# The beginning of a chunked linear-attention kernel: step 0's r and k in two transfers, and four r products behind the masks

## The chip, the core and the metric

The kernel runs on one core of a Trainium2 chip. The core has a matrix engine (TensorE, PE in the rows), two elementwise engines (VectorE, DVE; GpSimd, POOL), an activation engine (ScalarE, ACT) and a sync engine that issues transfers (SyncE, SP). Each engine runs its own instructions strictly in the order in which they were written and waits on semaphores for the others. Sixteen DMA engines move data between HBM and on-chip memory; SP and ACT both issue such transfers here, each on a queue of its own. The metric is the device time of one execution in microseconds (us).

## What is computed

A linear attention with decay over 768 tokens, for 4 batches and 8 heads of 48 dimensions, and then a mixture of experts over its output:

```python
for t in range(S):                        # S = 768
    cur = einsum('bhd,bhe->bhde', u * k[t], v[t])
    y[t] = einsum('bhd,bhde->bhe', r[t], state + cur)
    state = w[:, :, None] * state + einsum('bhd,bhe->bhde', k[t], v[t])
x = y as (3072 tokens, 384)
# tokens with x @ w_skip > 0 go to the expert argmax(x @ w_gate):
out = x + gate * (relu(x @ w1[e]) @ w2[e])
```

## The kernel before, in words

The attention is cut into chunks of 64 tokens. A step handles one chunk of two batches and all heads; there are 24 steps (NT), 12 for each pair of batches. The experts follow, about the second half of the time; the splitting of their weights and the routing run beside the steps.

A step n needs r and k from one transfer `dm{n}` (448 KB, both halves in one tile; three such buffers) and v from two transfers (`load_v`). Then:

- `prep_r(n)` (line 446, VectorE): `rd = r * table`, the table `w_d` of powers of the decay being built by VectorE at the start (lines 371 to 393) from the small input `wd`, loaded to `w_in`. `grow(1..3)` (line 362) make its three other quarters, which steps 1 to 3 need first. Four `rd` buffers.
- `bonus(n)`: `rd * u`, two heads at a time: two short activations on ScalarE (line 464), and one instruction on GpSimd (line 456) for the other half; in step 0 VectorE takes that half.
- `prep_k(n)` (line 469): `kd = k / table`, on GpSimd, for steps 0 and 1 on VectorE. Its end frees the buffer of `dm{n}` for `dm{n+3}`.
- `scores(n)` (line 496, TensorE): 16 small products into the one bank pair `ps_p`; `mask_scores(n)` (lines 508, 509, VectorE): two copies out of it, which have to be done before `scores(n+1)` writes it again.
- `within(n)` (line 550), `turn_x(n-1)` (line 619, transposes of the output of the step before), `turn_k` (482), `state` (520), `across(n)` (566): all on TensorE, in this order. ScalarE copies the result of `turn_x(n-1)` out of PSUM (line 623, "the x copy"). The first product of `across(n)` waits for that copy by a dependency written out by hand: `behind(mm, turned_x[n - 1])`. In every fourth step `gate_four` (636), which reads the copied x, stands between `state` and `across`.

The order in the loop over n decides what stands where on each engine. Before the change, iteration n is: `scores(n+1)`; `prep_r`, `bonus`, `prep_k` of step n+3; `within(n)`; `mask_scores(n+1)`; `turn_x(n-1)`, `turn_k(n+1)`, `state(n)`; `across(n)`. Iteration 0 prepares step 3 at its end. `warm` (line 271) fills TensorE with products of ones, at the very start and in a few gaps. `blank` (294) clears halves of the v buffers ahead of their first load.

Of the kernel before, what the change touches and what calls it, by code (L numbers as in the profile page):

```python
# [9 lines left out]
F32 = mybir.dt.float32  # L10
# [29 lines left out]
ADV = NB * NHP  # L40
BIG = 4 * N
NVK = 6
NWARM = 15
EARLY = 16
HURRY = 20
TURN = 9
# [14 lines left out]
def tile_wkv_moe(  # L61
# [199 lines left out]
    with ExitStack() as actx:  # L261
# [7 lines left out]
        def warm(k, to=ps_l):  # L269
            for _ in range(k):  # L270
                nc.tensor.matmul(to, ones[:, :P], ones, start=True, stop=True)
# [4 lines left out]
        NPW = 9  # L276
        pw = tab.tile([DR, NPW, 4 * NHP], F32, name="pw")
        w_in = tab.tile([DR, 4 * NHP], F32, name="w_in")
        nc.sync.dma_start(out=w_in, in_=wd)
        ub_sb = tab.tile([DR, NHP], F32, name="ub_sb")  # L280
        nc.scalar.dma_start(out=ub_sb, in_=ub)

# [9 lines left out]
        def blank(n, eng):  # L292
            for g in range(2):
                eng.memset(v_of(n)[g * C : (g + 1) * C, 1 - g], 0.0)

        def load_rk(n):
            d = ld.tile([DR, 2, NB * NHP * C], F32, tag="dm", name=f"dm{n}", bufs=3)
            nc.sync.dma_start(out=d.rearrange("p s (q c) -> p s q c", c=C), in_=dm[n // NSTEP, n % NSTEP])
            loaded[n] = (d, v_of(n))

        def load_v(n, k=2):
# [22 lines left out]
        nc.gpsimd.memset(am[0], 0.0)  # L324
        nc.gpsimd.memset(am[1], 0.0)
        nc.vector.memset(ps_s, 0.0)
        blank(0, nc.vector)

        def lower(name, op):
            t = tab.tile([P, C], I8, name=name)  # L330
# [12 lines left out]

        below = lower("below", ALU.is_gt)
        eye = lower("eye", ALU.is_equal)
        for j in range(1, 4):
            blank(j, nc.gpsimd)

        def behind(ins, name, reason="other rows of the array write the same quadrants"):
# [9 lines left out]
        def grow(sub, eng, after=None):  # L359
            if sub:  # L360
                src, j = (0, 6) if sub == 1 else (sub - 2, 7)
                ins = eng.tensor_tensor(
                    w_d[:, sub].rearrange("p s h c -> p (s h) c"),
                    w_d[:, src].rearrange("p s h c -> p (s h) c"),
                    pw[:, j, : 2 * NHP].unsqueeze(2).to_broadcast([DR, 2 * NHP, C]),
                    ALU.mult,
                )
                if after is not None:
                    behind(ins, after.ins.name, "r and k go first where both engines wait")
# [73 lines left out]
        def prep_r(n):  # L443
            d = loaded[n][0][:, 0].rearrange("p (b h c) -> p b h c", b=NB, h=NHP)
            rd = wk.tile([DR, NB, NHP, 2, C], F32, tag="rd", name=f"rd{n}", bufs=4)
            ins = nc.vector.tensor_tensor(  # L446
                rd[:, :, :, 0], d, w_d[:, n % NSUB, 0][:, None].to_broadcast([DR, NB, NHP, C]), ALU.mult
            )
            rds[n] = rd
            return ins  # L450

        def bonus(n, hps, eng=None):
            rd = rds[n]
            if eng is not None:
                h = slice(hps[0], hps[-1] + 1)
                eng.tensor_tensor(  # L456
                    rd[:, :, h, 1],
                    rd[:, :, h, 0],
                    uw[:, h][:, None, :, None].to_broadcast([DR, NB, len(hps), C]),
                    ALU.mult,  # L460
                )
                return
            for hp in hps:
                nc.scalar.activation(rd[:, :, hp, 1], rd[:, :, hp, 0], AF.Copy, scale=uw[:, hp : hp + 1])  # L464

        def prep_k(n, eng=None, after=None):
            d = loaded[n][0][:, 1].rearrange("p (b q) -> p b q", b=NB)
            kds[n] = wk.tile([DR, NB, NHP, C], F32, tag="kd", name=f"kd{n}", bufs=3)
            ins = (eng or nc.gpsimd).tensor_tensor(  # L469
                kds[n].rearrange("p b h c -> p b (h c)"),  # L470
                d,
                w_d[:, n % NSUB, 1].rearrange("p h c -> p (h c)")[:, None, :].to_broadcast([DR, NB, NHP * C]),
                ALU.mult,
            )
            if after is not None:
                behind(ins, after.ins.name, "r goes first where both engines wait")
            return ins
# [11 lines left out]
        def scores(n):  # L489
            kd, rd = kds[n], rds[n]  # L490
            for j in range(4):
                b, jj = divmod(j, 2)
                for a, g in FOUR:
                    h = slice(a * C, a * C + D)
                    hp = 2 * jj + g
                    mm = nc.tensor.matmul(  # L496
                        ps_p[g * C : (g + 1) * C, a, j * P : (j + 1) * P],
                        kd[h, b, hp, :],
                        rd[h, b, hp].rearrange("p s c -> p (s c)"),
                        start=True,  # L500
                        stop=True,
                    )
            return mm
# [414 lines left out]
        setup = setup_routes()  # L918
        prep_r(0)
        bonus(0, (0, 1))  # L920
        bonus(0, (2, 3), nc.vector)
        prep_k(0, nc.vector)
        scores(0)
        grow(1, nc.vector)
        square(7, nc.gpsimd)
        square(8, nc.gpsimd)
        prep_r(1)
        bonus(1, (0, 1))
        turn_k(0)
        bonus(1, (2, 3))  # L930
        k1 = prep_k(1, nc.vector)
        mask_scores(0)
        warm(4)
        state(0)
        grow(2, nc.gpsimd, k1)
        prep_k(2, after=prep_r(2))
        bonus(2, (0, 1, 2, 3))
        grow(3, nc.gpsimd)
        for n in range(NT):
            four = n % 4 == 0 and n > 0  # L940
            if 0 < n < NT - 4 and n % 2 == 0:
                load_v(n + 4)
            if n + 1 < NT:
                scores(n + 1)
            if 0 < n < NT - 3:
                prep_r(n + 3)
                bonus(n + 3, (0, 1))
                bonus(n + 3, (2, 3), nc.gpsimd)
                prep_k(n + 3)
            if n - 1 in WSPLIT:  # L950
                split_lo(0, WSPLIT.index(n - 1), nc.gpsimd)
            if 0 < n and n + 6 < NT:
                load_rk(n + 6)
            if n == NT - 2:
                step_route(4)
            else:
                tick()
            within(n)
            if n == NT - 1:
                vctx.close()  # L960
                scr.append(lctx.enter_context(tc.tile_pool(name="scr", bufs=4, side="right", reuse_waits="tile")))
                first = begin(0, "vkv", xhl0)
            if n + 1 < NT:
                mask_scores(n + 1)
                tick()
            if n > 0:
                turn_x(n - 1)
                if (n + 1) % NSTEP < NSTEP - 1 and n + 1 < NT:
                    turn_k(n + 1)
                state(n)  # L970
            if four:
                gate_four(n // 4 - 1)
            warm(FILL.get(n, 0))
            tick(0 if n < HURRY else 6)
            if n == NT - 1:
                next(first)
            if n == NT - 1:
                gate_four(n // 4)
            across(n)
            if n == 0:  # L980
                turn_k(1)
                prep_r(3)
                bonus(3, (0, 1))
                bonus(3, (2, 3), nc.gpsimd)
                prep_k(3)
                load_rk(6)
            if n == NT - 1:
                gate_back(n // 4)
            if n % NSUB == NSUB - 1 and n % NSTEP < NSTEP - 1:
                keep_state(n)  # L990
            if n == NT - 2:
                turn(ps_l[:, :DM].rearrange("p (c q) -> p c q", q=P), 0, xhl0[:, 0], xhl0[:, 1])
            if n != NSTEP:
                step_route(2)
            if n == NSTEP + 1:
                gate_back(n // 4 - 1)
            if four and n != NSTEP:
                gate_back(n // 4 - 1)
            if n < NT - 3 or n == NT - 1:
                step_route(4)  # L1000
            if n == NT - 1:
                step_route(4)
                tick(6)
                next(first)
                turn_x(n)
            step_route(1)
            tick(1 if n + 1 < NT else 6)
            if n in ends:
                routes.append([route(ends[n], n), 0, n])
            if 1 <= n < 5:  # L1010
                next(setup, None)
            if n in (1, 2):
                blank(n + 3, nc.gpsimd)
            if n in RAW0:
                load_expert(0, RAW0.index(n), 12)
            for j in RAW1.get(n, ()):
                load_expert(1, j, 6)
            for j in RAW2.get(n, ()):
                load_expert(2, j, 6)
            if n in WSPLIT:  # L1020
                split_hi(0, wpool, WSPLIT.index(n))
# [356 lines left out]
```

## Time and profile before

| | us |
|---|---|
| three timed runs, median (lowest to highest) | 271.28 (269.43 to 272.1) |
| the profiled execution, own time | 266.43 |
| its span, first to last instruction | 264.6 |
| TensorE busy, of that span | 251.7 (95%) |
| VectorE, ScalarE, GpSimd busy | 170.6, 139.4, 110.8 |
| granted TensorE clock, mean | 0.994 |

The page of the profile gives for each engine the busy time, then the span in 40 slices, then the chain of work that ended last, followed back from the end, and the costliest groups of instructions. For this change the first 35 us matter, and there the timelines of the single engines. A timeline row is: start, duration, engine, line, operation, tile written and tile read, number of instructions, and in brackets the idle time ahead of it with what ended it. A chain row is: start, duration on the chain, what. An operand is given as partitions x elements.

### The profile page before, as it was taken

What the parts mean: (1) busy time and instruction counts of PE and PEld (TensorE: products, weight loads), DVE (VectorE), ACT (ScalarE), POOL (GpSimd) and SP (SyncE); (2) the same over time, 40 slices, a digit from 0 to 9 for tenths busy, and PEclk for the clock granted to TensorE, in tenths of its full rate; (3) what the DMA queues carried; (4) which work ended last, traced back from release to release, by engine and by line L of the source; (5) the groups of instructions that cost most, each with busy time, mean ns of one, the idle gap of its engine ahead of it and who ended that gap; (6) DMA issues with size and microseconds to landing.
All of it is one profiled execution on the core that took longest, in us unless ns stands there. A gap on an engine that the chain in (4) does not pass through costs nothing.

```text
span 264.6 us, 8597 instructions
## 1 busy us (share of the span) xinstructions
PE 251.7 (95%) x3579; PEld 225.5 (85%) x3581; DVE 170.6 (64%) x382; ACT 139.4 (53%) x315; POOL 110.8 (42%) x128
## 2 busy tenths in 40 slices
PE   7799998989999999999999999999999999999990
PEld 2578887778888888877789999999999999999990
DVE  7768555568664877737865967948659477494300
ACT  2566565656766756444773916637258174491200
POOL 8579554474765655501778151220310403105011
PEclk9999999999999999999999999999999999999997
DMA  6998699988997888496399979185291670101000
GB/s 159 245 254 257 196 257 245 274 216 242 254 265 215 246 250 266 103 345 203 108 305 285 330 215 386 54 296 231 57 398 60 223 301 18 30 0 35 11 32 24
DMA packets 20864, 52.21 MB, mean 197 GB/s; under 512 B 3556, under 2 KB 10224, under 8 KB 20816
## 3 DMA queue, kind: packets, MB, share of 16 engines
q1 hardware_dynamic: 18240, 46.42, 58.2%
q0 software_dynamic: 2048, 5.14, 6.2%
q8 instruction: 30, 0.49, 0.8%
q14 instruction: 18, 0.15, 0.2%
q10 hardware_dynamic: 528, 0.02, 0.1%
HBM read 43.77 MB, written 8.36 MB: 197 GB/s over the span
## 4 chain that ended last, share of the span: by engine, by line
PE 85%; DMA 7%; DVE 2%; issue 1%; ACT 1%; SPq 1%; POOL 0%; POOLq 0%; DVEq 0%
PE ps_p L178 11%; PE ps_y L178 11%; PE ps_l L168 11%; PE ps_p L496 8%; PE ps_y L550 7%; PE ps_s L520 6%; PE ps_p L168 5%; PE ps_x L168 5%; PE ps_y L566 5%; DMA dm<-in_dm_dram 4%; PE ps_t L619 4%; PE ps_l L482 3%; DMA raw<-in_w_dram 2%; PE ps_t L636 2%; PE ps_y L233 2%
## 5 line engine op out<-in xcount | busy, mean ns | idle before, releaser
L187 POOL DMA_INDIRECT out_dram<-xg,sid x16 | 23.7, 1478 | 89.8 <-DVE xg L183 79.8
L129 DVE TENSOR_TENSOR wlo<-raw,whi 128x512 fp32r<-128x512 f32 x84 | 54.0, 685 | 2.1 <-ACT whi L124 2.0
L124 ACT CAST whi<-raw 128x512 fp32r<-128x512 f32 x96 | 54.7, 626 | 0.0
L446 DVE TENSOR_TENSOR rd<-dm,w_d 112x512 f32<-112x512 f32 x24 | 17.7, 740 | 17.9 <-PE ps_y L566 15.6
L168 PE MATMUL ps_l<-x,whi 128*128 128x232 f32 x168 | 28.9, 274 | 0.0
L469 POOL TENSOR_TENSOR kd<-dm,w_d 112x512 f32<-112x512 f32 x22 | 28.1, 1278 | 1.0 <-DVE rd L446 1.0
L496 PE MATMUL ps_p<-rd,kd 48*64 48x128 f32 x768 | 26.4, 273 | 1.5 <-issue 0.8
L138 POOL DMA_INDIRECT xg<-out_dram,gid x16 | 19.3, 1204 | 19.7 <-DMA raw<-in_w_dram 13.4
L456 POOL TENSOR_TENSOR rd<-rd,uw 112x256 f32<-112x256 f32 x21 | 12.9, 615 | 33.1 <-DVE rd L446 23.3
L168 PEld LDWEIGHTS ps_l<-x,whi 128*128 128x128 f32 x168 | 25.5, 192 | 0.0
L464 ACT ACTIVATE rd<-rd,uw 112x128 f32<-112x128 f32 x52 | 18.0, 396 | 11.2 <-DVE rd L446 10.8
L496 PEld LDWEIGHTS ps_p<-rd,kd 48*64 48x64 f32 x768 | 20.9, 133 | 3.3 <-issue 1.4
L168 PE MATMUL ps_l<-x,wlo 128*128 128x232 f32 x84 | 23.2, 276 | 0.0
L172 ACT ACTIVATE hh<-ps_p 128x464 fp32r<-128x464 f32 x7 | 3.9, 559 | 33.1 <-PE ps_p L168 33.1
L550 PE MATMUL ps_y<-vkv,am 128*64 128x96 f32 x384 | 21.1, 252 | 0.1
L508 DVE COPY_PREDICATED am<-below,ps_p 128x512 f32<-128x512 int8 x24 | 17.7, 736 | 4.7 <-PE ps_p L496 4.3
L550 PEld LDWEIGHTS ps_y<-vkv,am 128*64 128x64 f32 x384 | 16.6, 136 | 4.2 <-issue 2.9
L520 PE MATMUL ps_s<-vkv,kt 128*48 128x96 f32 x352 | 19.4, 251 | 0.8 <-issue 0.8
L623 ACT COPY x<-ps_t 128x384 f32<-128x384 f32 x23 | 11.0, 478 | 16.0 <-PE ps_t L619 15.9
L178 PE MATMUL ps_p<-whi,hh 128*128 128x384 f32 x56 | 19.4, 347 | 0.0
L178 PE MATMUL ps_y<-whi,hh 128*104 128x384 f32 x56 | 18.9, 338 | 0.0
L178 PE MATMUL ps_p<-whi,hl 128*128 128x384 f32 x56 | 18.9, 337 | 0.0
(239 smaller groups left out, 591.2 us busy)
## 6 DMA issues: line engine op xcount, KB each, us to landing
raw<-in_w_dram SPq DMA_DIRECT2D x16, 768.0 KB, 7.9
dm<-in_dm_dram SPq DMA_DIRECT2D x24, 448.0 KB, 5.3
raw<-in_w_dram SPq DMA_DIRECT2D x24, 256.0 KB, 5.5
raw<-in_w_dram SPq DMA_DIRECT2D x12, 512.0 KB, 5.5
out_dram<-xt SPq DMA_DIRECT2D x26, 192.0 KB, 4.3
vkv<-in_tok_dram SPq DMA_DIRECT2D x22, 192.0 KB, 4.5
vkv<-in_tok_dram SPq DMA_DIRECT2D x4, 96.0 KB, 6.5
out_dram<-xt SPq DMA_DIRECT2D x4, 96.0 KB, 4.3
```

Source lines behind the costliest of these rows:

```text
L124: nc.scalar.copy(wsp[e][0][:, s], raw[e][:, s])
L129: eng.tensor_tensor(lo[:, s], raw[e][:, s], hi[:, s].bitcast(F32), ALU.subtract)
L138: ins = nc.gpsimd.indirect_dma_start(out=xg[:m], out_offset=None, in_=out[:rows], in_offset=bass.IndirectOffsetOnAxis(ap=gid[:m, q : q + 1 ...
L168: nc.tensor.matmul(ph, w1[a][:, c, fs], x[:, c, b, :], start=(k == 0), stop=(k == 3 * NCC - 1))
L178: nc.tensor.matmul(py, a, b[:, f, :], start=(k == 0), stop=(k == 3 * NFC - 1))
L187: ins = nc.gpsimd.indirect_dma_start(out=out, out_offset=bass.IndirectOffsetOnAxis(ap=sid[:m, q : q + 1], axis=0), in_=xs.pop(q)[:m], in_o ...
L446: ins = nc.vector.tensor_tensor(rd[:, :, :, 0], d, w_d[:, n % NSUB, 0][:, None].to_broadcast([DR, NB, NHP, C]), ALU.mult)
L464: nc.scalar.activation(rd[:, :, hp, 1], rd[:, :, hp, 0], AF.Copy, scale=uw[:, hp : hp + 1])
L469: ins = (eng or nc.gpsimd).tensor_tensor(kds[n].rearrange("p b h c -> p b (h c)"), d, w_d[:, n % NSUB, 1].rearrange("p h c -> p (h c)")[:, ...
L496: mm = nc.tensor.matmul(ps_p[g * C : (g + 1) * C, a, j * P : (j + 1) * P], kd[h, b, hp, :], rd[h, b, hp].rearrange("p s c -> p (s c)"), st ...
L520: nc.tensor.matmul(s[a * C : a * C + D, j * 2 * D : (j + 1) * 2 * D], kt[:, j, a, :], v[:, j, a], start=i == 0 and j == 0, stop=True, skip ...
L550: nc.tensor.matmul(ps_y[b * C : (b + 1) * C, a, jj * 2 * D : (jj + 1) * 2 * D], am[n % 2][:, a, j * C : (j + 1) * C], v[:, j, a], start=jj ...
```

## The change

- `w_in` is loaded on ScalarE's queue, ahead of `ub_sb`, no longer on SP's; SP begins with r of step 0, then k of step 0, as two transfers of 224 KB where there was one of 448 KB.
- `prep_k(0)` is made in two halves (one per batch), with VectorE's half of step 0's bonus between them. `blank(0)` goes from VectorE to GpSimd, and `blank(2)` and `blank(3)` go behind `prep_k(1)`.
- `prep_k(1)` goes from VectorE to GpSimd, so `mask_scores(0)` directly follows `prep_r(1)` on VectorE; `grow(2)` goes from GpSimd to VectorE, behind that mask. All four bonuses of step 1 are together on ScalarE.
- `warm`: 13 products at the start where there were 15; 3 and 2 around `state(0)` where there were 4.
- In iterations 1 to 4 (`LEAD = 5`) the preparation of step n+3, steps 4 to 7, stands behind `mask_scores(n+1)`; before it stood ahead of it. It still stands ahead of `turn_x(n-1)`.

```diff
-NWARM = 15
+LEAD = 5
+NWARM = 13
...
-        nc.sync.dma_start(out=w_in, in_=wd)
+        nc.scalar.dma_start(out=w_in, in_=wd)
...
-            nc.sync.dma_start(out=d.rearrange("p s (q c) -> p s q c", c=C), in_=dm[n // NSTEP, n % NSTEP])
+            for s in (slice(0, 1), slice(1, 2)) if n == 0 else (slice(0, 2),):
+                nc.sync.dma_start(
+                    out=d[:, s].rearrange("p s (q c) -> p s q c", c=C), in_=dm[n // NSTEP, n % NSTEP, :, s]
+                )
...
-        blank(0, nc.vector)
...
-        for j in range(1, 4):
+        for j in range(2):
             blank(j, nc.gpsimd)
...
         prep_r(0)
         bonus(0, (0, 1))
+        prep_k(0, nc.vector, part=slice(0, 1))
         bonus(0, (2, 3), nc.vector)
-        prep_k(0, nc.vector)
+        prep_k(0, nc.vector, part=slice(1, 2))
         scores(0)
+        turn_k(0)
         grow(1, nc.vector)
         square(7, nc.gpsimd)
         square(8, nc.gpsimd)
-        prep_r(1)
-        bonus(1, (0, 1))
-        turn_k(0)
-        bonus(1, (2, 3))
-        k1 = prep_k(1, nc.vector)
+        k1 = prep_k(1, after=prep_r(1))
+        for j in range(2, 4):
+            blank(j, nc.gpsimd)
+        bonus(1, (0, 1, 2, 3))
         mask_scores(0)
-        warm(4)
+        warm(3, ps_t)
         state(0)
-        grow(2, nc.gpsimd, k1)
+        warm(2, ps_t)
+        grow(2, nc.vector)
         prep_k(2, after=prep_r(2))
         bonus(2, (0, 1, 2, 3))
         grow(3, nc.gpsimd)
+
+        def prepare(n):
+            prep_r(n)
+            bonus(n, (0, 1))
+            bonus(n, (2, 3), nc.gpsimd)
+            prep_k(n)
...
-            if 0 < n < NT - 3:
-                prep_r(n + 3)
-                bonus(n + 3, (0, 1))
-                bonus(n + 3, (2, 3), nc.gpsimd)
-                prep_k(n + 3)
+            if LEAD <= n < NT - 3:
+                prepare(n + 3)
...
                 mask_scores(n + 1)
+                if 0 < n < LEAD:
+                    prepare(n + 3)
+                    load_rk(n + 6)
                 tick()
             if n > 0:
                 turn_x(n - 1)
```

VectorE's order from step 0's r to the masks of step 3, before. Numbers behind a name are a tile's own (`rd_201` to `rd_412` are rd of steps 0 to 5, `am` are the masked scores of even and odd steps):

```order
L446 TENSOR_TENSOR rd_227<-dm_128,w_d 112x8x64
L469 TENSOR_TENSOR kd_239<-dm_128,w_d 112x512
L508 COPY_PREDICATED am_149<-below,ps_p 128x512
L509 COPY_PREDICATED am_149<-eye,ps_p 128x512
L446 TENSOR_TENSOR rd_257<-dm_135,w_d 112x8x64
L508 COPY_PREDICATED am_150<-below,ps_p 128x512
L509 COPY_PREDICATED am_150<-eye,ps_p 128x512
L446 TENSOR_TENSOR rd_302<-dm_139,w_d 112x8x64
L446 TENSOR_TENSOR rd_327<-dm_143,w_d 112x8x64
L508 COPY_PREDICATED am_149<-below,ps_p 128x512
L509 COPY_PREDICATED am_149<-eye,ps_p 128x512
```

The same place in the changed kernel (its lines are 3 to 5 higher; rd of steps 1 to 4 are `rd_229`, `rd_258`, `rd_303`, `rd_338`):

```order
L449 TENSOR_TENSOR rd_229<-dm_127,w_d 112x8x64
L513 COPY_PREDICATED am_148<-below,ps_p 128x512
L514 COPY_PREDICATED am_148<-eye,ps_p 128x512
L365 TENSOR_TENSOR w_d<-w_d,pw 112x512
L449 TENSOR_TENSOR rd_258<-dm_134,w_d 112x8x64
L513 COPY_PREDICATED am_149<-below,ps_p 128x512
L514 COPY_PREDICATED am_149<-eye,ps_p 128x512
L449 TENSOR_TENSOR rd_303<-dm_138,w_d 112x8x64
L513 COPY_PREDICATED am_148<-below,ps_p 128x512
L514 COPY_PREDICATED am_148<-eye,ps_p 128x512
L449 TENSOR_TENSOR rd_338<-dm_142,w_d 112x8x64
```

k of step 1 is gone from VectorE and a quarter of the table has come; r of step 4 stood ahead of the masks of step 2 and now stands behind them.

ScalarE's order in iterations 1 and 2, in the changed kernel. `rd_338` and `rd_423` are bonuses of steps 4 and 5; `x_350` at L628 is the x copy (line 623 before):

```order
L467 ACTIVATE rd_338<-rd_338,uw 112x2x64 x2
L628 COPY x_350<-ps_t 128x3x128
L489 COPY kt_356<-ps_l 128x384
L543 COPY sblk_192<-ps_s 112x384
L584 COPY xt_295<-ps_y 128x2x4x48
L467 ACTIVATE rd_423<-rd_423,uw 112x2x64 x2
L628 COPY x_350<-ps_t 128x3x128
```

On ScalarE these rows stand in the same order as before: the bonus of step n+3 is ahead of the x copy of step n-1 in both kernels.

GpSimd's order behind the squares, in the changed kernel (kd of steps 1, 2 and 3 are `kd_231`, `kd_260`, `kd_308`):

```order
L474 TENSOR_TENSOR kd_231<-dm_127,w_d 112x512
L295 MEMSET vkv_122 64x384 x4
L474 TENSOR_TENSOR kd_260<-dm_134,w_d 112x512
L365 TENSOR_TENSOR w_d<-w_d,pw 112x512
L459 TENSOR_TENSOR rd_303<-rd_303,uw 112x2x2x64
L474 TENSOR_TENSOR kd_308<-dm_138,w_d 112x512
```

The first two of these rows are new at this place; the table quarter in it is the one that r of step 3 needs.

## Rows read from the trace of the kernel before

**Rows 1.** Page: shares of the span in the chain that ended last

```profile
PE 85%; DMA 7%; DVE 2%; issue 1%; ACT 1%; SPq 1%; POOL 0%; POOLq 0%; DVEq 0%
```

**Rows 2.** Chain that ended last, first 31 us: start, us, what

```profile
0.80 0.40 SPq L279
...
1.25 4.47 DMA dm<-in_dm_dram
...
9.57 6.61 DMA dm<-in_dm_dram
...
16.27 1.30 DVE rd L446
...
18.29 0.37 ACT x L623
...
18.70 0.68 PE ps_y L566 x32
...
20.27 0.81 PE ps_y L550 x16
...
22.75 0.61 PE ps_y L566 x32
...
24.25 0.81 PE ps_y L550 x16
```

**Rows 3.** Timeline of VectorE

```profile
3.13 0.18 DVE L371 TENSOR_SCALAR pw<-w_in 112x16 f32<-112x16 f32 x1
...
5.34 0.15 DVE L393 TENSOR_TENSOR uw<-ub_sb,pw 112x4 f32<-112x4 f32 x1
5.82 0.69 DVE L446 TENSOR_TENSOR rd<-dm,w_d 112x512 f32<-112x512 f32 x1 [0.33 <-DMA dm<-in_dm_dram]
6.55 0.42 DVE L456 TENSOR_TENSOR rd<-rd,uw 112x256 f32<-112x256 f32 x1
6.89 0.70 DVE L469 TENSOR_TENSOR kd<-dm,w_d 112x512 f32<-112x512 f32 x1
7.51 0.69 DVE L362 TENSOR_TENSOR w_d<-w_d,pw 112x512 f32<-112x512 f32 x1
8.24 0.69 DVE L446 TENSOR_TENSOR rd<-dm,w_d 112x512 f32<-112x512 f32 x1
...
24.31 0.73 DVE L508 COPY_PREDICATED am<-below,ps_p 128x512 f32<-128x512 int8 x1
25.08 0.74 DVE L509 COPY_PREDICATED am<-eye,ps_p 128x512 f32<-128x512 int8 x1
```

**Rows 4.** Timeline of ScalarE

```profile
17.59 0.69 ACT L464 ACTIVATE rd<-rd,uw 112x128 f32<-112x128 f32 x2 [1.79 <-DVE rd L446]
18.20 0.46 ACT L623 COPY x<-ps_t 128x384 f32<-128x384 f32 x1
```

**Rows 5.** Timeline of GpSimd

```profile
3.88 2.66 POOL L294 MEMSET vkv<- 64x384 f32 x6
...
11.66 1.27 POOL L469 TENSOR_TENSOR kd<-dm,w_d 112x512 f32<-112x512 f32 x1 [1.01 <-DVE rd L446]
12.90 1.04 POOL L362 TENSOR_TENSOR w_d<-w_d,pw 112x512 f32<-112x512 f32 x1
15.16 0.62 POOL L456 TENSOR_TENSOR rd<-rd,uw 112x256 f32<-112x256 f32 x1 [1.22 <-DVE rd L446]
15.73 1.28 POOL L469 TENSOR_TENSOR kd<-dm,w_d 112x512 f32<-112x512 f32 x1
```

**Rows 6.** DMA issues: tile, queue, count, KB each, median us to landing

```profile
w_in<-in_wd_dram SPq DMA_DIRECT2D x1, 7.0 KB, 1.6
ub_sb<-in_ub_dram ACTq DMA_DIRECT2D x1, 1.8 KB, 1.7
wg_sb<-in_wg_dram ACTq DMA_DIRECT2D x1, 13.5 KB, 6.3
```

**Rows 7.** TensorE's waits behind 20 us: us in total, times, longest

```profile
PE ps_s L520 <- issue: 0.8, 1, 0.8
```

More of the change, by code (lines that the diff above doesn't have):

```diff
@@ L464, in bonus, with prep_k @@
                 nc.scalar.activation(rd[:, :, hp, 1], rd[:, :, hp, 0], AF.Copy, scale=uw[:, hp : hp + 1])
-        def prep_k(n, eng=None, after=None):
+        def prep_k(n, eng=None, after=None, part=slice(0, NB)):
             d = loaded[n][0][:, 1].rearrange("p (b q) -> p b q", b=NB)
-            kds[n] = wk.tile([DR, NB, NHP, C], F32, tag="kd", name=f"kd{n}", bufs=3)
+            if part.start == 0:
+                kds[n] = wk.tile([DR, NB, NHP, C], F32, tag="kd", name=f"kd{n}", bufs=3)
+            table = w_d[:, n % NSUB, 1].rearrange("p h c -> p (h c)")[:, None, :]
             ins = (eng or nc.gpsimd).tensor_tensor(
-                kds[n].rearrange("p b h c -> p b (h c)"),
-                d,
-                w_d[:, n % NSUB, 1].rearrange("p h c -> p (h c)")[:, None, :].to_broadcast([DR, NB, NHP * C]),
+                kds[n].rearrange("p b h c -> p b (h c)")[:, part],
+                d[:, part],
+                table.to_broadcast([DR, part.stop - part.start, NHP * C]),
                 ALU.mult,
@@ L944, in tile_wkv_moe @@
                 scores(n + 1)
-            if 0 < n < NT - 3:
-                prep_r(n + 3)
-                bonus(n + 3, (0, 1))
-                bonus(n + 3, (2, 3), nc.gpsimd)
-                prep_k(n + 3)
+            if LEAD <= n < NT - 3:
+                prepare(n + 3)
             if n - 1 in WSPLIT:
                 split_lo(0, WSPLIT.index(n - 1), nc.gpsimd)
-            if 0 < n and n + 6 < NT:
+            if LEAD <= n < NT - 6:
                 load_rk(n + 6)
@@ L981, in tile_wkv_moe @@
                 turn_k(1)
[L982 to L985, printed above, removed]
+                prepare(3)
                 load_rk(6)
```

## Prediction, made before the changed kernel was run

> **What bounds the kernel now.** Read first the shares of the chain that ended last [rows 1]: 85% of the span is TensorE, so from some point on only TensorE's own work counts, and what moves that point moves the end. Then read that chain from its start [rows 2]. Until 18.70 it is not TensorE: it goes through the transfer of r and k of step 0, through that of step 4 (`dm4`, issued at 9.57, landed at 16.18), then through `rd` of step 4 on VectorE (16.27, 1.30 long), the bonus and the x copy on ScalarE, to `across(1)` at 18.70. Behind that one TensorE row follows the other. So the change is measured at two places: when `across(1)` begins, and whether TensorE still runs without gaps behind it. Third, read ScalarE [rows 4]: the bonus of step 4 waited 1.79 us for VectorE, and the x copy, which `across(1)` waits for, stood behind that bonus. ScalarE works in order, so the x copy can't overtake. This queue is what decides here.
>
> **Steps 2 to 4: r behind the masks.** Take a step of before in which TensorE does not wait. `scores` end at 20.27 on the chain and `across(2)` follows at 22.75, 2.48 us later, all TensorE work [rows 2]. The x copy had time enough, because `rd` of step n+3 ran while `scores` ran. In the changed order `rd` comes behind the masks, and the masks can't begin before `scores` end. Counted from the end of `scores`: first mask 0.06 later (24.25 on the chain, 24.31 on VectorE) [rows 2, 3]; the second mask starts 0.77 after the first and takes 0.74, so the masks end at +1.57 [rows 3]; `rd` 0.69, of which 0.06 overlaps as between neighbours in that view, ends at +2.20; the bonus starts 0.03 later, the x copy 0.61 after the bonus, and takes 0.46 [rows 4], so it ends at +3.30; `across` begins 0.04 later, as 18.66 to 18.70 [rows 2], at +3.34. TensorE has 2.48 us of work for this: it idles about 0.85 us. That holds in iterations 2, 3 and 4 (in 4 it is `gate_four` that waits, which reads the copied x): 3 x 0.85 = **2.55 us lost**. The bounds are narrow, since all are rows of the same instructions: 2.4 to 2.8. From iteration 5 on the old order is back. What is late next on TensorE is everything, by the same amount. The loads of later steps (`dm{n+6}` waits for `kd` of step n+3) come up to a step later too, but `rd` there waits for the masks anyway, so I price that at nothing; without that cover it would cost the wait for the landing.
>
> **The beginning, up to `across(1)`.** Two chains can set it, and the later one counts.
>
> *The transfers.* Between the landings of `dm0` (1.25 + 4.47 = 5.72) and `dm4` (16.18) [rows 2] lie by program order and shapes 4 x 448 KB of r and k, 4 x 96 and 2 x 192 KB of v: 2560 KB, 2.62 MB in 10.46 us, 250 GB/s. That stream has no gap to close. The change removes no byte from it; it only starts at 0.80, where `w_in` stood, and not at 1.25: 0.45 us earlier. `dm4` lands at 15.73. Then `rd` of step 4 starts 0.09 later, at 15.82, takes 0.69 if GpSimd leaves it alone (see below), and 1.14 further (0.03, 0.61, 0.46, 0.04, as above) is `across(1)` at 17.65. Of the same stream: 448 KB take 1.83 us, so of `dm0`'s 4.47 us 2.64 are a fixed start, and r of step 0 alone lands at 0.80 + 2.64 + 0.92 = 4.36.
>
> *The engines.* Let W be the landing of `w_in`. VectorE's table starts at W + 0.05 (before: 3.13, since `blank(0)` stood ahead; that memset is gone from VectorE) and ends 2.40 later (3.13 to 5.34, 0.15, and a handover) [rows 3]. From the start of `rd` of step 0 to the end of that of step 1: 0.73, three half instructions at 0.34 (the step of the 256-element bonus, 6.55 to 6.89), 0.73 for `grow(1)` (7.51 to 8.24), 0.69, together 3.17 [rows 3]. So step 1's r ends at W + 5.62. Then GpSimd, in its new order: `kd` of step 1 at 1.24 (11.66 to 12.90), four memsets at 0.443 (2.66 for six), `kd` of step 2 at 1.24, the table's last quarter 1.04 [rows 5], with a handover 5.32: W + 10.94. `rd` of step 3 waits for that quarter, and on VectorE the masks of step 2 stand behind it: they begin at W + 11.6 and end at W + 13.1. `rd` of step 4 now meets `kd` of step 3 on GpSimd, which ends at W + 11.66 + 0.04 + 0.57 + 1.28 = W + 13.55 [rows 5]. Before, `rd` took 1.30 and not 0.69 and ended 0.55 us after that `kd` (15.73 + 1.28 = 17.01, against 17.57) [rows 2, 5]; so here it ends at W + 14.10, and `across(1)` begins at W + 15.24.
>
> *What is W?* Before, `w_in` was first on SP's queue and took 1.6 us. On ScalarE's queue the rows give two bounds: the tiny `ub`, first there with no large transfer beside it, 1.7 us, so W = 2.5; and r of step 0, which is issued at the same moment and whose landing (4.4) a 7 KB transfer should not outlast. I take the middle, 3.5. A far bound is `wg`, 13.5 KB issued beside two large transfers, 6.3 us [rows 6], W = 7.1. `across(1)` is then at 17.74 (W 2.5), **18.74 (W 3.5)**, 19.64 (W 4.4) or 22.34 (W 7.1), against 18.70: -1.0, **0.0**, +0.9, +3.6.
>
> *The other edits.* Halves of k, an earlier `turn_k(0)`, `mask_scores(0)` without `kd` of step 1 ahead of it (0.7 us), 13 and 5 warm products for 15 and 4: all end before one of the two chains does, so nothing; uncovered, the halves would cost one instruction's fixed part, 2 x 0.34 against 0.62 [rows 3]. `kd` of step 1 frees `dm4`'s buffer on GpSimd at W + 6.9 (10.4, against 9.57 before) [rows 2]; the stream has work queued until 15.73, so nothing there either.
>
> **Sum**, against the profiled execution's 266.43: 0.0 + 2.55 = +2.6, so 269.0. Its time lies 4.85 below the median of the three timed runs; on that median it is **273.9**.
>
> The Trainium skill, page "DMA: Bandwidth & Descriptors", section "Queues, rings and completion order", says that a DMA engine goes round its queues and drains a whole packet, some 9 to 17 descriptors, of one before it switches. By that rule r's 112 rows, 7 for each of 16 engines, would all go ahead of `w_in` where they come first, and the sum would be +3.5. The trace agrees as far as `wg` shows it: 6.3 us beside large transfers.
>
> **Rivals.**
> - *The table's source goes behind r of step 0* (W = 4.4, or a little above). For it: `wg`'s 6.3 against `ub`'s 1.7 [rows 6]. Against it: 7 KB issued at the same moment. +0.9 + 2.55 = +3.5: 274.8. If it fares like `wg` altogether, +3.6 + 2.55 = +6.2: 277.5.
> - *Later waits pay some of it back.* TensorE has two waits of 0.8 us behind 30 us that nothing in the profile explains ("issue") [rows 7]. If these are instructions that come at their own time, a later TensorE finds them there: 2.6 - 1.6 = +1.0, down to 0.0 with W = 2.5: 272.3. Against it: they may as well move along.
> - *Faster: the x copy is not what holds TensorE.* If `across` went on without it, the masks that no longer stand behind a transfer would let TensorE run from `scores(2)`. That needs `kd` of step 2, at W + 9.9 on GpSimd, 12.4 with W = 2.5; from there 3.4 us of work (0.9 for `scores`, 2.48 behind them) bring `across(1)` at 15.8, no gaps follow, and it is -2.9: 268.4. It decides at 2.48 us: an x copy that ends sooner than that after `scores` costs nothing. Against it: +3.30 above, from rows that differ little, and the wait at 18.70, which the chain gives to the x copy.
>
> **How the numbers follow.** Forecast with W from 2.5 to 4 (+1.6 to +3.1): 0.52. Source behind r: 0.20. Like `wg`: 0.06. Paid back: 0.14. Faster: 0.08. The time is that of the first, 273.9. One per cent is 2.7 us, about what a measurement of this kernel can tell from no change. Slower by more: a third of the forecast (W above 3.6), 0.17, with 0.20 and 0.06: 0.43. Faster by more: the last, 0.08. Within: 0.49. The range leaves out the faster case and that like `wg` (0.14): from the paid-back case at its lowest, 271.3, to 274.8, each widened by 0.8 for medians of runs that lie from 269.43 to 272.1: 270.5 to 275.6. The forecast's own is 272.9 to 274.4.
>
> **What would show it.** In ScalarE's timeline of the changed kernel, the x copies of iterations 2 to 4 directly behind a bonus that waited for `rd`; in TensorE's, gaps of 0.8 to 0.9 us ahead of `across(2)`, `across(3)` and `gate_four`, released by the x copy, and none from iteration 5 on. `w_in`'s time to landing gives W, and with it `across(1)` at W + 15.2, or 17.7 at the earliest. `rd` of step 4 ends about 0.55 behind `kd` of step 3. I am wrong if `across(2)` follows `scores(3)` by 2.5 us, or if `across(1)` comes before 17.

## The result and the profile after

| | before | after |
|---|---|---|
| median of 12 runs each, us | 268.87 | 270.88 |
| lowest and highest, us | 266.05, 273.03 | 268.75, 275.52 |
| ratio, 95% interval | | 1.011 (1.0075 to 1.0145) |
| profiled execution, us | 266.43 | 269.76 |
| its span, us | 264.6 | 268.1 |

By the ratio the change makes the kernel about 1.1% slower, some 3.0 us. The ratio leaves out every execution that took over 1.5% longer than the fastest of its kernel (274.08 and 275.52 us of after, some of before, and in a later run one of 1172.65 us), while the medians, 2.0 us apart, hold them all. The forecast was +2.6 us: 269.0 for the profiled execution, which took 269.76, and 273.9 on 271.28, the median of the three runs known then. These three are among the twelve of before, whose median is 268.87, so the median of after lies below 273.9 although the difference is larger than 2.6.

The chain that ended last, after (start, us, what), answers to [rows 2]:

```profile
0.81 3.17 DMA w_in<-in_wd_dram
...
9.60 1.28 POOL kd L474
10.90 6.42 DMA dm<-in_dm_dram
17.42 0.72 DVE rd L449
...
18.87 0.37 ACT x L628
19.28 0.68 PE ps_y L571 x32
...
23.72 0.37 ACT x L628
24.14 0.68 PE ps_y L571 x32
...
147.43 1.08 issue
```

Before, the chain came to `across(1)` at 18.70 and was nearly all TensorE's from there on. Now it comes there at 19.28, and behind that it goes back to the x copy on ScalarE in iterations 2 to 4. TensorE's timeline shows what that costs; a row is start, us, engine, line, operation, tile, and in brackets the idle time ahead of it and what ended it:

```profile
19.28 0.68 PE L571 MATMUL ps_y<-sblk,rd 48*64 48x48 f32 x32 [1.35 <-ACT x L628]
...
24.14 0.68 PE L571 MATMUL ps_y<-sblk,rd 48*64 48x48 f32 x32 [0.81 <-ACT x L628]
...
28.99 0.68 PE L571 MATMUL ps_y<-sblk,rd 48*64 48x48 f32 x32 [0.81 <-ACT x L628]
...
33.90 0.86 PE L641 MATMUL ps_t<-x,wg_sb 128*32 128x128 f32 x24 [0.87 <-ACT x L628]
...
78.89 0.87 PE L501 MATMUL ps_p<-rd,kd 48*64 48x128 f32 x20 [0.57 <-issue]
...
84.32 0.72 PE L555 MATMUL ps_y<-vkv,am 128*64 128x96 f32 x12 [0.28 <-issue]
```

`across(2)`, `across(3)` and `gate_four` (line 641) each wait 0.8 to 0.9 us, 2.49 us together. The loss is a little larger than the idle time: from one `across` to the next takes 4.85 us (24.14 to 28.99), where before it took 3.97 (22.75 to 26.72 in the chain), 0.88 more. From iteration 5 on the x copy ends only one short wait, of 0.18 us at 63.63 us, and before had the same at 63.07. VectorE and ScalarE of after show the cause, in the order that was forecast: masks behind `scores`, `rd` behind the masks, bonus behind `rd`, x copy behind the bonus. VectorE:

```profile
20.92 0.73 DVE L513 COPY_PREDICATED am<-below,ps_p 128x512 f32<-128x512 int8 x1 [2.77 <-PE ps_p L501]
21.69 0.73 DVE L514 COPY_PREDICATED am<-eye,ps_p 128x512 f32<-128x512 int8 x1
22.32 0.68 DVE L449 TENSOR_TENSOR rd<-dm,w_d 112x512 f32<-112x512 f32 x1
```

ScalarE of after, which answers to [rows 4]:

```profile
18.18 0.69 ACT L467 ACTIVATE rd<-rd,uw 112x128 f32<-112x128 f32 x2 [1.78 <-DVE before L417]
18.78 0.46 ACT L628 COPY x<-ps_t 128x384 f32<-128x384 f32 x1
...
23.03 0.69 ACT L467 ACTIVATE rd<-rd,uw 112x128 f32<-112x128 f32 x2 [2.52 <-DVE rd L449]
23.63 0.46 ACT L628 COPY x<-ps_t 128x384 f32<-128x384 f32 x1
```

Where the 3.5 us of span went, from the starts of the same stages in the two timelines of TensorE:

| stage | before | after | later by |
|---|---|---|---|
| `across(1)` | 18.70 | 19.28 | 0.58 |
| `scores(6)`, behind the three gaps | 32.28 | 35.57 | 3.29 |
| the `across` with the wait of 0.18 | 63.07 | 63.63 | 0.56 |
| the gate products near 85 | 84.57 | 86.63 | 2.06 |
| the first matmuls on the gathered rows (`ps_t<-ident,xg`) | 129.21 | 131.29 | 2.08 |
| end of the span | 264.6 | 268.1 | 3.5 |

Up to 36 us the forecast holds almost row by row, but for the landings of `w_in` and of step 4's transfer. Behind that the difference falls and rises again, through waits that the profile puts down to "issue", as those of [rows 7]: before has three between 36 and 63 us (0.79, 0.23 and 0.76 us), after none there, but two at 78.89 and 84.32 and one of 1.08 at 147.43. The stages that hold them are longer by more than the idle time shown: from one `scores` to the next takes 3.97 us where nothing waits and 4.97 where the 0.57 lies.

### The profile page after: what moved, and what is told of

It reads as the page before. It is cut to its first block, busy times and chain, and to the rows that moved or that the text cites. A ratio compares the mean times of both kernels' runs of the same rounds, so it can differ in the third digit from the quotient of the medians.

```text
span 268.1 us, 8601 instructions
## 1 busy us (share of the span) xinstructions
PE 252.1 (94%) x3580; PEld 225.3 (84%) x3580; DVE 169.0 (63%) x381; ACT 138.6 (52%) x315; POOL 109.8 (41%) x130
## 4 chain that ended last, share of the span: by engine, by line
PE 86%; DMA 5%; DVE 3%; issue 2%; ACT 2%; POOL 1%; POOLq 0%; DVEq 0%; ACTq 0%
PE ps_p L179 11%; PE ps_y L179 11%; PE ps_l L169 11%; PE ps_p L501 8%; PE ps_y L555 7%; PE ps_s L525 6%; PE ps_p L169 5%; PE ps_x L169 5%; PE ps_y L571 5%; PE ps_t L624 4%; PE ps_l L487 3%; DMA dm<-in_dm_dram 2%; PE ps_t L641 2%; PE ps_y L234 2%; PE ps_l L212 1%
## 5 line engine op out<-in xcount | busy, mean ns | idle before, releaser
L474 POOL TENSOR_TENSOR kd<-dm,w_d 112x512 f32<-112x512 f32 x23 | 29.3, 1275 | 2.4 <-DVE rd L449 2.4
L449 DVE TENSOR_TENSOR rd<-dm,w_d 112x512 f32<-112x512 f32 x24 | 16.5, 689 | 15.7 <-PE ps_y L571 14.5
L139 POOL DMA_INDIRECT xg<-out_dram,gid x16 | 18.2, 1141 | 19.7 <-DVE em L865 15.4
L628 ACT COPY x<-ps_t 128x384 f32<-128x384 f32 x23 | 10.9, 475 | 15.4 <-PE ps_t L624 15.2
L179 PE MATMUL ps_y<-wlo,hh 128*104 128x384 f32 x56 | 18.9, 337 | 0.0
```

Source lines behind the costliest of these rows:

```text
L139: ins = nc.gpsimd.indirect_dma_start(out=xg[:m], out_offset=None, in_=out[:rows], in_offset=bass.IndirectOffsetOnAxis(ap=gid[:m, q : q + 1 ...
L179: nc.tensor.matmul(py, a, b[:, f, :], start=(k == 0), stop=(k == 3 * NFC - 1))
L474: ins = (eng or nc.gpsimd).tensor_tensor(kds[n].rearrange("p b h c -> p b (h c)")[:, part], d[:, part], table.to_broadcast([DR, part.stop ...
```

## The experiments

All are edits of the changed kernel, but for the second, which is one of the kernel before. `scores(6)` tells what the beginning and the three gaps did together, before the waits of 40 us and later come in.

| run | `across(1)` | `scores(6)` | span | ratio to before (95%) |
|---|---|---|---|---|
| before | 18.70 | 32.28 | 264.6 | 1 |
| after | 19.28 | 35.57 | 268.1 | 1.011 (1.0075 to 1.0145) |
| after, second execution | 19.30 | 35.59 | 266.5 | |
| preparation in its old place | 18.03 | 31.85 | 265.9 | 1.0031 (0.9992 to 1.0069) |
| before, with that move alone | 19.16 | 35.45 | 267.6 | 1.0127 (1.0069 to 1.0185) |
| x copy ahead of the bonus | 17.48 | 33.65 | 264.7 | 1.0006 (0.9966 to 1.0046) |
| preparation behind `across` | 17.88 | 31.70 | 263.3 | 0.9987 (0.9943 to 1.0031) |
| source first on SP | 19.53 | 37.63 | 268.9 | 1.0187 (1.0119 to 1.0256) |
| the same, TensorE kept busy | 19.32 | 35.62 | 268.6 | 1.0103 (1.0036 to 1.017) |
| source first, preparation behind `across` | 16.83 | 31.74 | 262.9 | 0.9973 (0.9937 to 1.001) |
| kd of step 1 on VectorE | 19.66 | 35.95 | 268.0 | 1.0091 (1.0049 to 1.0132) |
| source first, preparation behind `across`, kd on VectorE | 17.62 | 32.40 | 265.5 | 0.9983 (0.9935 to 1.0032) |

**The loss undone, and the loss alone.** The first run takes the move of r of steps 4 to 7 out of the change and leaves the rest:

```diff
-LEAD = 5
+LEAD = 1
```

> The changed kernel with LEAD = 1: r, bonus and k of steps 4 to 7 stand ahead of the masks again, all else as changed. Theory (the x copy behind a bonus that waits for r behind the masks costs 0.8 us in each of steps 2 to 4): the three gaps of 0.81, 0.81 and 0.87 us go, across(1) stays near 19.3 because r of step 4 still waits for its transfer; span 268.1 - 2.5 = 265.6, time about 1.004 of the kernel before. Rival (the loss sits in the beginning, the place of r is harmless): span stays near 268.

The second makes that move alone, in the kernel before (`LEAD = 5`, `prepare` and the two places that call it, with all else as before):

> The kernel before with that one part alone: r, bonus and k of steps 4 to 7 behind the masks. Theory: r of step 4 waits for the masks of step 2, which end at 17.3, so across(1) at 19.1 (18.7 before), and three gaps of about 0.83 us follow: span 264.6 + 0.4 + 2.5 = 267.5, 1.011 of the kernel before. Rival (loss in the beginning): span 264 to 265, since the masks of step 2 no longer wait for the transfer of step 4.

TensorE of the second run; line 567 is `across`, line 637 `gate_four`:

```profile
19.16 0.68 PE L567 MATMUL ps_y<-sblk,rd 48*64 48x48 f32 x32 [0.81 <-ACT x L624]
24.01 0.68 PE L567 MATMUL ps_y<-sblk,rd 48*64 48x48 f32 x32 [0.81 <-ACT x L624]
28.87 0.68 PE L567 MATMUL ps_y<-sblk,rd 48*64 48x48 f32 x32 [0.81 <-ACT x L624]
33.78 0.86 PE L637 MATMUL ps_t<-x,wg_sb 128*32 128x128 f32 x24 [0.87 <-ACT x L624]
```

The gaps come and go with this one move. With it undone the span was 265.9, for 265.6 expected, but `across(1)` came at 18.03 and not near 19.3: step 4's transfer landed at 15.76 in that execution, and r of step 4 no longer stood behind the masks. The move carries the whole loss: 1.0127 by itself, against 1.011 for the change. The rest of the change brings `scores(6)` 0.43 us earlier and moves the time by +0.3%, with an interval that holds no change.

**Whose order makes the gaps.** In the next run masks still come ahead of r on VectorE; only ScalarE's order differs, since the preparation stands behind `turn_x(n-1)`, whose x copy so comes ahead of the bonus:

```diff
             if n > 0:
                 turn_x(n - 1)
+                if n < LEAD:
+                    prepare(n + 3)
+                    load_rk(n + 6)
```

(the same three lines behind `mask_scores(n + 1)` are taken out.)

> The changed kernel with the preparation of steps 4 to 7 moved behind turn_x(n-1), so that ScalarE copies x ahead of the bonus; r stays behind the masks on VectorE. Theory (it is the x copy's place in ScalarE's order): no gap ahead of across(1) to across(3) and gate_four; across(1) directly behind state(1), near 17.9 for 19.28, and 2.5 us less in steps 2 to 4: span 268.1 - 1.4 - 2.5 = 264.2, about 0.998 of the kernel before. Rival (r's late place itself holds TensorE, by a buffer or by k): gaps stay, span 267 to 268.

The three gaps are gone although r still comes behind the masks. That shows ScalarE's order, not the late r itself, to be what TensorE waits for. The gain did not come whole, as TensorE of this run shows:

```profile
19.00 0.33 PE L571 MATMUL ps_y<-sblk,rd 48*64 48x48 f32 x7 [0.92 <-issue]
...
21.08 0.88 PE L555 MATMUL ps_y<-vkv,am 128*64 128x96 f32 x16 [0.84 <-ACT xt L584]
```

A later copy in ScalarE's queue, that of `xt`, stood behind the bonus of step 4, which here waited for a transfer that landed at 18.39. So the preparation was put behind `across(n)`, where every copy of the step is ahead of it:

```diff
             across(n)
             if n == 0:
                 turn_k(1)
+            if n < LEAD:
+                prepare(n + 3)
+                load_rk(n + 6)
```

> The changed kernel with the preparation of steps 4 to 7 written behind across(n) of steps 0 to 3, so that every copy on ScalarE that the turns of a step need stands ahead of bonus of step n + 4. Theory (ScalarE's order is what TensorE waits for at across(1) to across(3) and at the first gate product): the gaps of 0.81 to 0.87 us ahead of those stages are gone, as they were with the x copy alone moved ahead, and the wait of 0.84 us for the xt copy in step 2 that stood in that run goes too. Span 263.6 if the transfer of step 4 lands between 16 and 18 us, some 1 us below the kernel before; ratio 0.996. Rival (the preparation is now late itself): r of step 4 ends so late that scores(4) waits for it; span 264.7 or more.

From `across(1)` at 17.88 to `scores(6)` at 31.70 the profile shows no wait of TensorE; only `scores(4)` takes longer, 1.31 us for 1.07. The span is 263.3, 0.3 below what was expected. The time is that of before within the interval: the expected 0.996 lies in it, and so does 1.

**The table's source.** The change puts `w_in` on ScalarE's queue behind the start of r. Here it goes first on SP, all else as changed:

```diff
-            nc.scalar.dma_start(out=w_in, in_=wd)
+            nc.sync.dma_start(out=w_in, in_=wd)
```

> The changed kernel with the table's source first on SP's queue again, all else as changed. Theory (its landing at 3.98 makes the beginning late): it lands at 2.4, r of step 0 starts near 4.9 and not at 6.48, step 4's transfer is issued near 9.3 and not at 10.9, across(1) near 18.2; the three gaps stay: span 268.1 - 1.1 = 267.0. Rival (the stream of transfers alone sets across(1)): across(1) stays at 19.3 and the span at 268.1. Second rival (the source is what costs everything): span 265.

This was a miss. The source lands 1.8 us from its issue, and the first scores start 1.45 us earlier than in the changed kernel, yet `across(1)` came later and the kernel was slower still. The chain of this run, and then TensorE's rows:

```profile
9.84 7.76 DMA dm<-in_dm_dram
...
17.69 0.69 DVE rd L449
...
19.53 1.10 PE ps_y L571 x32
```

```profile
15.76 0.87 PE L525 MATMUL ps_s<-vkv,kt 128*48 128x96 f32 x16
19.53 1.10 PE L571 MATMUL ps_y<-sblk,rd 48*64 48x48 f32 x32 [2.90 <-ACT x L628]
20.41 1.95 PE L501 MATMUL ps_p<-rd,kd 48*64 48x128 f32 x32
```

Step 4's transfer landed at 17.60, no earlier than in the changed kernel (17.32), so an earlier TensorE only waited longer for the x copy behind it: 2.90 us. Behind that wait everything on TensorE took longer, `scores(3)` 1.95 us and not 1.07, until about 25 us. Of the three gaps that were expected to stay, the one ahead of `across(2)` is missing: the x copy had time while TensorE was slow. The stretches of this run (us of the stretch, PE busy with matmuls, granted clock, DMA share, GB/s) tell why:

```profile
16.00:18.00 2.00, 0.63 (x16) 1.00 1.04 225
18.00:20.00 2.00, 0.47 (x18) 0.67 1.10 199
20.00:22.00 2.00, 2.00 (x56) 0.50 0.96 221
22.00:24.00 2.00, 2.00 (x25) 0.50 0.95 269
24.00:26.00 2.00, 2.00 (x21) 0.62 0.94 291
26.00:28.00 2.00, 2.00 (x79) 1.00 0.39 85
```

TensorE had been idle from about 16.6 to 19.5; the granted clock was at 0.50, the lower of its two levels (1.2 and not 2.4 GHz), from 20 to 24 us, and partly so in the stretches beside these. To test that this was the extra loss, the next run fills the wait with 12 products into a bank that nothing reads:

```diff
+            warm(12 if n == 1 else 0, ps_x)
             across(n)
```

> The run with the source first on SP, with 12 more products on TensorE ahead of across(1), into a bank that nothing reads, so that TensorE is busy in most of the 2.9 us for which it waited there. Nothing else differs. Theory (that run lost its time to the clock, which was granted at 0.50 to 0.67 from 18 to 26 us behind the wait): the granted clock stays at 1.00 from 10 to 40 us, scores(3) runs 0.9 us and not 1.73, span 267 or less against 268.9. Rival (the fall of the clock had another cause, or came in that execution alone): the clock falls here as well, or the ratio to the kernel before stays at 1.019.

The same stretches in this run:

```profile
16.00:18.00 2.00, 2.00 (x20) 1.00 1.08 229
18.00:20.00 2.00, 1.81 (x46) 1.00 1.01 233
20.00:22.00 2.00, 2.00 (x52) 1.00 0.52 130
22.00:24.00 2.00, 1.36 (x22) 1.00 0.86 260
24.00:26.00 2.00, 1.82 (x72) 1.00 0.93 266
26.00:28.00 2.00, 2.00 (x37) 1.00 0.91 228
```

The clock stays at 1.00, `scores(3)` is 0.89 long in the chain again and not 1.73, and `scores(6)` starts at 35.62 and not at 37.63, with `across(1)` 0.21 earlier. So the clock cost that run some 1.8 us, net of the gap ahead of `across(2)` that it hid. It was not that one execution alone: the mean granted clock of the six with the source first on SP is 0.975 to 0.991, of the six with TensorE kept busy 0.988 to 0.998. The span missed its 267: it lost 1.42 and 0.99 us in "issue" waits at 53.70 and 59.72, which the other did not have. The ratios point the same way (1.0103 against 1.0187), but their intervals overlap. With the clock mended, an earlier source is still worth nothing here.

It is worth something only where ScalarE's order is mended too:

> The same order as in the run with the preparation behind across(n), and the table's source issued first on SP, ahead of the two transfers of step 0. Theory: the source lands near 2.6 us as it did when it went first on SP, and the first scores start near 6.2 us instead of 7.7; without the wait of 2.9 us at across(1), which came from ScalarE's order behind a late transfer of step 4, the 1.3 us of the earlier beginning are kept: across(1) at 16.2 to 16.8 us, span 262.3, ratio 0.990. Rival (step 4's transfer, which landed between 15.8 and 18.4 us, is now what scores(4) or masks wait for): the beginning is early but TensorE waits later; span 263.5 or more.

`across(1)` came at 16.83, 1.05 earlier than with the source on ScalarE's queue, and TensorE lost it again in the next step, in `scores(4)`:

```profile
21.30 0.72 PE L501 MATMUL ps_p<-rd,kd 48*64 48x128 f32 x17
23.04 0.66 PE L501 MATMUL ps_p<-rd,kd 48*64 48x128 f32 x15 [1.02 <-issue]
```

The ratio of 0.990 was missed. At 0.9973 its ratio is the lowest of all, but it is not shown to be faster than before.

**kd of step 1.** The prediction priced its move to GpSimd at nothing. Undone:

```diff
-        k1 = prep_k(1, after=prep_r(1))
+        prep_r(1)
+        k1 = prep_k(1, nc.vector)
```

> The changed kernel with kd of step 1 back on VectorE behind r of step 1, which undoes one part. The prediction priced this move at nothing. Theory A (the price is nothing since TensorE then waits for the transfer of step 4 or for r of step 4 as before): kd of step 1 ends near 10.2 us and no longer at 10.87, kd of step 3 on GpSimd ends near 16.3 us and no longer at 17.60, but across(1) still starts between 18.9 and 19.3; span within 0.4 us of 268.1, gaps 0.81, 0.81, 0.87 unchanged. Theory B (GpSimd's row of kd sets the end of r of step 4, which ran 0.54 us behind kd of step 3): r of step 4 ends near 17.0 us where the transfer has landed by 16.2, across(1) at 18.0 to 18.3, span 267.0, ratio 0.4% below that of the changed kernel.

Theory A has the span right (268.0, gaps of 0.82, 0.82 and 0.88), but neither had the rows, and `across(1)` at 19.66 is later than both allowed. GpSimd has one product less, yet `kd` of step 3 started later, at 16.69 and not at 16.32. VectorE's timeline of this run:

```profile
9.44 0.68 DVE L474 TENSOR_TENSOR kd<-dm,w_d 112x512 f32<-112x512 f32 x1
10.05 0.73 DVE L513 COPY_PREDICATED am<-below,ps_p 128x512 f32<-128x512 int8 x1
10.88 0.73 DVE L514 COPY_PREDICATED am<-eye,ps_p 128x512 f32<-128x512 int8 x1
11.50 0.67 DVE L365 TENSOR_TENSOR w_d<-w_d,pw 112x512 f32<-112x512 f32 x1
12.21 0.69 DVE L449 TENSOR_TENSOR rd<-dm,w_d 112x512 f32<-112x512 f32 x1
...
17.37 1.14 DVE L449 TENSOR_TENSOR rd<-dm,w_d 112x512 f32<-112x512 f32 x1
```

On VectorE kd pushes the table's third quarter from 10.90 to 11.50, and with it r of step 2, and GpSimd waits for that r before it can take up kd of step 2. So VectorE was the engine with no room; the move to GpSimd brings `across(1)` 0.38 us earlier (19.28 against 19.66), too little for the time to tell (1.011 against 1.0091). All three edits together:

> All three edits together: preparation of steps 4 to 7 behind across(n), the table's source first on SP, kd of step 1 on VectorE. Theory: across(1) near 16.8 us as with the first two, because there TensorE ran without a wait from 9.1 us on and kd of step 1 is not waited for; span 262.5, ratio 0.995. Rival (waits for instructions, which came at other places in each run, take back what the beginning gains): across(1) at 16.8 and a span of 263.5 or more.

This gave `across(1)` at 17.62, not 16.8: r of step 1 started at 8.38, behind a wait of 0.99 us for its transfer, and TensorE lost 0.88 and 0.85 us in "issue" waits up to 55 us. It is no better than its parts.

**The same instructions again.**

> The changed kernel once more, one look. Theory (the landing of step 4's transfer differs between executions of the same instructions by up to 2.6 us, since the rate of the stream does): it lands anywhere between 15.7 and 18.4 us, across(1) starts 2 us behind its landing where it lands late and near 18.0 where it lands early, and the gaps of 0.81 to 0.87 us ahead of across(2), across(3) and the first gate product are there again. Rival (the landing is set by the order of the instructions): it lands at 17.3, as in the first profile.

The three gaps, 0.81, 0.81 and 0.87, were there again, and `across(1)` at 19.30, 0.02 from the first. Where VectorE waited for step 4's transfer in the first execution, it did not in the second; `rd` was slow instead. GpSimd and VectorE of the second:

```profile
16.33 1.28 POOL L474 TENSOR_TENSOR kd<-dm,w_d 112x512 f32<-112x512 f32 x1
```

```profile
17.00 1.16 DVE L449 TENSOR_TENSOR rd<-dm,w_d 112x512 f32<-112x512 f32 x1
```

The transfer, issued at 10.92, landed 5.2 us later, at 16.1, where it had landed at 17.32 in the first execution, and r ended at 18.16, against 18.14. By the transfers' chain `across(1)` would have come near 18.0; so the engines' chain alone gives 19.30, and in the first execution both chains ended together. The expectation that it would be near 18.0 with an early landing was wrong, and so was the notion behind it that the transfer alone sets it. The waits of 0.57 and 0.28 us at 78.90 and 84.34 stand at the same instructions in both executions; that of 1.08 at 147 is in the first alone. It is most of the 1.6 us between the two spans.

## Why the prediction was right, step by step

- **The three gaps, 2.55 us.** Right, for the reason given: 0.81, 0.81 and 0.87, 2.49 together, each released by the x copy; by the length of an iteration, 0.88 each. The second run has them with this move alone, the one with the x copy ahead of the bonus loses them by ScalarE's order alone.
- **No gaps from iteration 5 on.** Right.
- **The engines' chain, `across(1)` at W + 15.24.** Right: `w_in` landed at 3.98, which gives 19.22, and it was 19.28. What it was built of holds too: `rd` of step 4 ends 0.54 us behind `kd` of step 3 (18.14 behind 17.60); in the second execution 18.16 is 0.55 behind 17.61, and with kd of step 1 on VectorE 18.51 is 0.54 behind 17.97. One piece does not follow W. VectorE's first table instruction, 0.18 us long before [rows 3], started between 3.81 and 4.03 in five executions of the changed beginning and ended at 4.30 to 4.32 in all of them, when GpSimd's first memset of a v buffer, begun at 3.87, ends too. So the second execution, with W = 3.85 (19.09 by the sum), was no earlier: 19.30. Whether the memset holds that instruction was not tested.
- **W = 3.5, the middle of 2.5 and 4.4.** Mis-sized by 0.48: `w_in` took 3.17 us from issue to landing, where it had taken 1.6 at the head of SP's queue [rows 6]. The bounds held. In six executions of the changed beginning it landed between 3.74 and 4.00, so the middle was a poor choice and not bad luck. With 3.98 the sum is +0.5 + 2.55, or 269.5, against 269.76. What the rows show is the rival "source behind r", with r earlier than its estimate of 4.36: in the four of these executions whose traces have its landing, r of step 0 landed 2.8 us after its issue, at 3.6, and `w_in` 0.1 to 0.3 us behind it. So W fell just inside the forecast's 2.5 to 4, but by the rival's order. Such an execution is the second one; r's transfer, and `w_in` in the chain:

```profile
L300 SPq DMA_DIRECT2D dm<-in_dm_dram x1: 402/402/402, 0.8 to 0.8; - x1
DMA to landing us min/median/max: 2.8/2.8/2.8
...
0.81 3.04 DMA w_in<-in_wd_dram
```

  By the Trainium skill, "DMA: Bandwidth & Descriptors", "Queues, rings and completion order", a whole packet of r would go first. The order of the landings agrees; no run here shows the packets. All landings of `w_in` lie far below that like `wg`.
- **The transfers' chain, `dm4` at 15.73.** Too early: 17.32. The stretches from 5 to 20 us moved 225, 224 and 220 GB/s, where before moved 242, 257 and 245, so "the stream has no gap, and only starts earlier" is not a forecast of its end. How it was to count, as landing + 0.09 + 0.69 + 1.14, is confirmed: with the source first on SP 17.60 and 17.40 give 19.52 and 19.32, and `across(1)` came at 19.53 and 19.32. That the term did not spoil the sum is luck, since the engines' chain ended at the same time. In the second execution the landing was at 16.1, near the forecast.
- **`kd` of step 1 at nothing.** Near enough: 0.38 us in favour of the change, by a way that I had not seen (VectorE's room, above). Its other price was as said: `dm4` was issued later, at 10.90, but in the runs with issues at 9.84, 10.50 and 10.90 it landed at 17.60, 18.39 and 15.76, so the issue does not set the landing.
- **The rival "later waits pay some of it back".** In part true, and I gave it too little thought rather than too little chance. Between 36 and 63 us the difference fell from 3.29 to 0.56 us, because the waits of before are not there in after; then other waits took 1.5 back. The ratio, at +1.1%, says that on the whole little was paid back. In the sum of +2.6 these waits were taken to move along, and they did not; they came at other places, to much the same total in the profiled execution (1.78 us before, 0.57 + 0.28 + 1.08 = 1.93 after).
- **The time, 273.9, and the range.** Here luck helped. The base of 271.28 was 2.4 above the median of the twelve runs, so 270.88 lies below the forecast's own 272.9 to 274.4, and inside 270.5 to 275.6 only because the range reached down for later waits that pay back. The difference, some +3.0, lies inside +1.6 to +3.1. Of the chances, the largest went to a change within one per cent, 0.49; it came out at 1.1%, among the 0.43.
- **The rival "faster".** Excluded by the x copies in the chain. Its clock was not thought of at all: an early TensorE that waits 2.9 us for the x copy can lose the clock besides.

**What stays open.** Why the "issue" waits fall where they fall. They add some 0.6 to 2.6 us up to 87 us in these runs, they differ between kernels whose instructions differ by a few rows, and one came in one execution of two. The page of the profile counts 30 transfers of instructions on one queue, 0.49 MB together, 16 KB each, in every run. The Trainium skill, "Runtime: NRT & Kernel Launch", "Instruction fetch mechanics", says that an engine fetches its program in blocks of that size through a DMA queue while it runs, and calls the cost mostly hidden. The counted transfers agree with the block; that these waits are such blocks coming late is a guess and was not tested. Nor was it tested why the same instructions moved 220 GB/s in one execution, from 15 to 20 us, and 247 in another.

## What to carry to other kernels

When work is moved behind something that takes long, look at every in-order queue that it is a part of: here r moved on VectorE, and what stopped TensorE was a copy on ScalarE that stood behind r's last piece. Count from an event to the waiting instruction along rows that exist already; that gave a gap of 0.85 where 0.81 to 0.87 came, while the step that was guessed between two bounds was off by half a microsecond. And read an effect at the stage where it arises, not at the end of one profile: in these runs the rest of the span, from `scores(6)` on, differed by 3 us (230.9 to 234.1), in stages that no edit here touches.

## What the runs showed of the hardware that was not expected

- An idle TensorE can cost twice. After 2.90 us without work the granted clock fell to 0.50, and some 1.8 us went by the clock; waits of 1.35 and 1.50 us at the same place left it at 1.00.
- A 7 KB transfer that took 1.6 to 1.8 us at the head of SP's queue took 2.9 to 3.2 us on ScalarE's queue, issued together with a transfer of 224 KB, and landed 0.1 to 0.3 us behind that one in the four executions that show both.
- The same transfer of 448 KB (`dm4`), issued at 10.9 in two executions of the same kernel, landed 5.2 us later in one and 6.42 us later in the other; in the other runs of the changed beginning that show it, 4.8 to 7.9 us later.
